# Fifteen small loads of 1 to 15 rows, each with its own semaphore, between the last two parts of w_down

## The chip, the cores and the metric

The kernel runs on one core of one Trainium2 chip. Such a core has five engines that run side by side, each from its own list of instructions: TensorE (PE in the profile; PEld is its loading of weights), VectorE (DVE), ScalarE (ACT), GpSimd (POOL) and SyncE (SP). Sixteen DMA engines move data between the chip's memory (HBM) and the on-chip memory (SBUF). Engines wait for each other, and for DMAs, on semaphores. The metric is the time of one execution in microseconds (us) on the device. Three runs of the kernel before took 1309.85 to 1310.14 us, the median is 1309.92 us.

## The reference

One decoding step of a transformer block, in float32, for a batch of 2 with one new position each: attention over a cache of 8192 positions in 32 heads of 128, and then a gated feed-forward layer. The model width D is 512, the inner width F of the feed-forward layer is 1792.

```
h  = x + attention(layernorm(x))        # q = layernorm(x) @ wq, then per batch and head:
                                        #   softmax(q . k_cache / sqrt(128)) @ v_cache
                                        # and the heads' outputs, side by side, @ wo
h2 = h + (silu(n @ w_gate) * (n @ w_up)) @ w_down,   n = layernorm(h)
```

k_cache and v_cache are 2 x 32 x 8192 x 128 numbers each. Every number of them is used once, so nearly all the traffic is cache.

## The kernel before, in words

The kernel is written by hand as five lists of steps, one for each engine. `do` adds a step to an engine's list, and gives it a semaphore to raise if one is named; `wait` adds a wait to the list. A DMA raises its semaphore by 16 in all when it has landed. `emit` writes the lists out in order. So each engine works strictly in the order in which its steps were added, and that of SyncE's loads is the order of the list `loads`.

The attention goes in 32 rounds (U = 32), two heads of one batch entry a round. A round reads 8 MB of k_cache and 8 MB of v_cache. VectorE multiplies the keys with the query (L418) and sums up (L427), TensorE helps with the softmax (L318 to L323) and multiplies the probabilities with the values (L328). There are two buffers for keys, `kslot`, and one for values, `vslot`; the last round's values go to a key buffer. SyncE waits until a buffer is free (`freed`, L579) and then issues the load into it (L580).

Behind the cache, in the same list, come the weights of the end: wo in three parts into `vslot` (5, 2 and 1 MB), w_gate and w_up in two parts each into a key buffer (1.75 MB each), and w_down in five parts into the other (`WD`, L190: 1 MB, 1 MB, 768 KB, 512 KB and 256 KB). Each part has a semaphore of its own, which `alone` makes, so that TensorE can start on a part as soon as it has landed. Before the first part of a weight SyncE waits for the step that frees its buffer (`after`, L202); the first part of w_down has to wait for TensorE's multiplication with the values of the last round (L328).

The end of the computation is a chain: the last round's output, the multiplication with wo (L477), a layernorm (L234 to L252), w_gate and w_up (L511), and w_down (L563), where TensorE waits for the semaphore of each part. VectorE copies the result (L574), and SyncE and ScalarE store one half of it each (L587). SyncE then waits for both stores and clears all semaphores, which are numbered without a gap (L593 to L596).

The lines around the change are those that put w_down's parts into the list of loads, and those that issue the list:

Of the kernel before, what the change touches and what calls it, by code (L numbers as in the profile page):

```python
# [13 lines left out]
class Program:  # L14
# [16 lines left out]
    def wait(self, engine, *points):  # L31
        for s, value in points:
            if self.known[engine].get(s, 0) < value:
                self.known[engine][s] = value
                self.steps[engine].append(lambda e, s=s, v=value: e.wait_ge(s, v))  # L35

    def do(self, engine, fn, sem=None, by=1):

        if sem is None:
            self.steps[engine].append(fn)  # L40
            return None
        self.count[sem] += by
        self.steps[engine].append(lambda e: fn(e).then_inc(sem, by))
        return sem, self.count[sem]
# [8 lines left out]
def decode_block(nc, x, k_cache, v_cache, wq, wo, w_gate, w_up, w_down, out):  # L53
    B, _, D = x.shape
    _, H, S, DH = k_cache.shape
# [21 lines left out]
    def sbuf(name, *shape, align=32):  # L77
        return nc.alloc_sbuf_tensor(name, list(shape), F32, align_bytes=align).ap()
# [51 lines left out]
    wait, do = g.wait, g.do  # L130
# [6 lines left out]
    def alone(name):  # L137
        return g.sem(name)
# [3 lines left out]
    landed = {}  # L142
    freed = {}
    loads = []
# [36 lines left out]
    for e, (c, n) in enumerate(WF):  # L181
        src, c0 = (w_gate, c) if c < DC else (w_up, c - DC)
        loads.append((
            ("wf", 0), e,
            wf_t[:, c * F : (c + n) * F],
            src.rearrange("(p c) f -> p (c f)", p=P)[:, c0 * F : (c0 + n) * F],
            alone(f"wf{e}"),
        ))
    wd_t = v_last
    WD = ((0, 4), (4, 4), (8, 3), (11, 2), (13, 1))  # L190
    for e, (c, n) in enumerate(WD):
        loads.append((
            ("wd", 0), e,
            wd_t[:, c * D : (c + n) * D],
            w_down.rearrange("(p c) m -> p (c m)", p=P)[:, c * D : (c + n) * D],
            alone(f"wd{e}"),
        ))
    count = {}
    for item, e, dst, src, sem in loads:
        count[sem] = count.get(sem, 0) + 16  # L200
# [31 lines left out]
    def layernorm(src, ready):  # L232
        wait("vector", *ready)
        p = do("vector", lambda e: e.bn_stats(stats, src), s_dve)  # L234
        wait("vector", p)
        p = do("vector", lambda e: e.bn_aggr(mv, stats), s_dve)
        wait("vector", p)
        p = do("vector", lambda e: e.tensor_scalar(ve, mv[:, 1:2], EPS, None, op0=OP.add), s_dve)
        wait("gpsimd", p)
        p = do("gpsimd", lambda e: e.tensor_tensor(rstd, ve, mhalf, op=OP.pow), s_pool)  # L240
        wait("vector", p)
        p = do(
            "vector",
            lambda e: e.tensor_scalar(y, src, mv[:, 0:1], rstd, op0=OP.subtract, op1=OP.mult),
            s_dve,
        )
        normed = p
        wait("tensor", p, ident_done)
        for c in range(DC):
            p = do(  # L250
                "tensor",
                lambda e, c=c: e.transpose(yt[:, c, :], y.rearrange("b (p c) -> b c p", c=DC)[:, c, :], ident[:B, :B]),  # L252
                s_pe if c == DC - 1 else None,
            )
        return normed, p

    _, p = layernorm(xs, [(x_in, 16)])
# [151 lines left out]
    for i in range(U):  # L409
        m, b = divmod(i, B)  # L410
        parts = 4 if i == 0 else 2
        n = NJ // parts
# [164 lines left out]
    for item, e_, dst, src, sem in loads:  # L577
        if item in after:
            wait("sync", freed[after[item]])  # L579
        do("sync", lambda e, dst=dst, src=src: e.dma_start(dst, src), sem, 16)  # L580
    stored = []
    for b, engine in enumerate(("sync", "scalar")):
        wait(engine, res_done)
# [52 lines left out]
```

## Time and profile before

| | us |
|---|---|
| median of three runs | 1309.92 (1309.85 to 1310.14) |
| the profiled execution, its own time | 1309.8 |
| its span, first to last instruction | 1308.5 |
| VectorE busy in it | 1131.7 |
| TensorE matmuls busy in it | 434.9 |
| loads of w_down issued | 1270.4 to 1276.9 |
| SyncE waits for the result, until | 1306.4 |

The profile is one execution, recorded by the hardware. Times within it count from the start of the span. The profile's page shows shares by engine and by slices of the span; the chain of waits follows the work that ended last back to what released it; the timeline shows instructions in order, with the time that an engine sat idle before them and what ended that in square brackets. "SPq" and "ACTq" are the sequencers of SyncE and ScalarE when they issue a DMA, and the length of such a line is the time that the issue took, not that of the transfer. The landing of a DMA is when its semaphore has been raised in full; the profile gives the time from issue to landing by load. The windows give the busy time of the engines, TensorE's granted clock, the share of time in which the DMA engines were busy, and GB/s, for a stretch.

### The profile page before, as it was taken

The numbers are of one execution on the slowest core, as the hardware profiler recorded it, in microseconds if no ns is written. First come the engines' busy times: TensorE is split into PE (matmuls) and PEld (weight loads), VectorE is DVE, ScalarE is ACT, GpSimd is POOL, SyncE is SP. The second block draws the span as 40 slices with busy tenths as digits, with TensorE's granted clock in tenths as the row PEclk, the third lists the DMA queues.
The fourth block names the chain that finished last, engine by engine and source line by source line (L and its number), as shares of the span: only waits on it lengthen the run. The fifth ranks groups of instructions, "written<-read, shape, count | busy, mean of one in ns | idle before, by whom it ended". The sixth has DMA issues, their size and how long they took to land.

```text
span 1308.5 us, 6711 instructions
## 1 busy us (share of the span) xinstructions
PE 434.9 (33%) x2952; PEld 135.4 (10%) x2952; DVE 1131.7 (86%) x250; ACT 80.4 (6%) x271; POOL 2.9 (0%) x13
## 2 busy tenths in 40 slices
PE   3633223333223333311333321233332233332177
PEld 1210001011001011100101100001100010110022
DVE  2999888889888889988888988888998888898841
ACT  0100000000000000000000000000000000000010
POOL 0000000000000000000000000000000000000000
PEclk9865566666556666656666656666655666665578
DMA  9999999999999999999999999999999999999998
GB/s 401 440 439 443 425 445 423 443 423 445 421 445 429 437 439 429 443 425 443 423 445 421 445 429 437 441 427 443 425 441 425 441 425 441 433 435 443 425 422 370
DMA packets 11550, 564.79 MB, mean 432 GB/s; under 512 B 1290, under 2 KB 1298, under 8 KB 1684
## 3 DMA queue, kind: packets, MB, share of 16 engines
q1 hardware_dynamic: 11528, 564.67, 99.7%
q8 instruction: 5, 0.08, 0.0%
q14 instruction: 5, 0.04, 0.0%
q10 hardware_dynamic: 12, 0.01, 0.0%
HBM read 564.66 MB, written 0.00 MB: 432 GB/s over the span
## 4 chain that ended last, share of the span: by engine, by line
DMA 56%; DVE 43%; PE 1%; issue 0%; SPq 0%; ACT 0%; DVEq 0%
DMA kslot<-in_A_k_cache_dram 48%; DVE kslot L418 21%; DVE s L427 21%; DMA kslot<-in_A_v_cache_dram 3%; DMA kslot<-in_B_w_down_dram 3%; DMA vslot<-in_A_wq_dram 2%; PE opart L328 1%; PE wide L291 0%; DVE gm L371 0%; DVE r L397 0%; PE bank L563 0%; SPq L580 0%; ACT qsb L302 0%; DVE kslot L574 0%; DVEq L35 0%
## 5 line engine op out<-in xcount | busy, mean ns | idle before, releaser
L418 DVE TENSOR_TENSOR kslot<-kslot,qsb 128x8192 f32<-128x8192 f32 (+1 forms) x66 | 555.9, 8422 | 126.8 <-DMA kslot<-in_A_k_cache_dram 103.7
L427 DVE TENSOR_REDUCE s<-kslot 128x64 f32<-128x8192 f32 (+1 forms) x66 | 555.5, 8417 | 0.1
L328 PE MATMUL opart<-vslot,pz 128*8 128x512 f32 x1984 | 285.2, 740 | 250.4 <-DMA vslot<-in_A_v_cache_dram 250.4
L320 PE MATMUL bank<-gm,nscale 1*64 1x1 f32 x64 | 11.8, 251 | 361.1 <-DVE gm L371 361.1
L328 PEld LDWEIGHTS opart<-vslot,pz 128*8 128x8 f32 x1984 | 55.2, 103 | 454.3 <-DMA vslot<-in_A_v_cache_dram 253.0
L318 PE MATMUL bank<-ident,m 128*1 128x128 f32 x64 | 18.7, 395 | 164.3 <-DVE m L435 164.3
L320 PEld LDWEIGHTS bank<-gm,nscale 1*64 1x64 f32 x64 | 9.1, 200 | 377.1 <-DVE gm L371 377.1
L340 PE MATMUL bank<-rdiag,osb 128*128 128x2 f32 x256 | 33.7, 254 | 23.6 <-ACT osb L404 23.6
L399 ACT ACTIVATE rdiag<-fold,r 128x8 f32<-128x8 f32 x32 | 9.6, 301 | 484.6 <-DVE r L397 484.6
L378 ACT ACTIVATE nb<-bank 128x1 f32<-128x1 f32 x32 | 5.5, 171 | 550.6 <-PE bank L321 550.6
L340 PEld LDWEIGHTS bank<-rdiag,osb 128*128 128x128 f32 x256 | 31.0, 191 | 53.3 <-ACT osb L404 53.3
L291 PE MATMUL wide<-vslot,osb 128*64 128x512 f32 x128 | 29.9, 631 | 17.2 <-DMA vslot<-in_A_wq_dram 17.2
L323 PE MATMUL bank<-rs,sides 128*128 128x1 f32 x64 | 18.8, 363 | 41.5 <-ACT pz L384 41.5
L384 ACT ACTIVATE pz<-s,nb 64x128 f32<-64x128 f32 x64 | 25.5, 399 | 1.4
L404 ACT ACTIVATE osb<-opart 128x512 f32<-128x512 f32 x32 | 19.1, 596 | 73.6 <-PE opart L328 73.6
L323 PEld LDWEIGHTS bank<-rs,sides 128*128 128x128 f32 x64 | 16.1, 313 | 44.2 <-ACT pz L384 44.2
L318 PEld LDWEIGHTS bank<-ident,m 128*1 128x1 f32 x64 | 2.7, 81 | 167.9 <-DVE m L435 167.9
L291 PEld LDWEIGHTS wide<-vslot,osb 128*64 128x64 f32 x128 | 10.4, 146 | 35.9 <-issue 35.9
L234 DVE BATCH_NORM_STATS2 ln_stats<-attn 2x6 f32<-2x512 f32 x1 | 0.7, 686 | 13.1 <-PE attn L490 13.1
L384 ACT ACTIVATION_READ_ACCUMULATOR pz<-s,nb 64x1 f32 x64 | 11.8, 184 | 0.0
L321 PE MATMUL bank<-gm,nscale 1*64 1x1 f32 x64 | 11.8, 251 | 0.0
L450 DVE TENSOR_TENSOR om<-oT,quarter 128x256 f32<-128x256 f32 x1 | 0.4, 425 | 11.4 <-ACT oT L406 11.4
(60 smaller groups left out, 105.1 us busy)
## 6 DMA issues: line engine op xcount, KB each, us to landing
kslot<-in_A_k_cache_dram SPq DMA_DIRECT2D x4, 2048.0 KB, 32.9
vslot<-in_A_wo_dram SPq DMA_DIRECT2D x1, 5120.0 KB, 22.0
kslot<-in_B_w_gate_dram SPq DMA_DIRECT2D x2, 1792.0 KB, 29.4
kslot<-in_B_w_up_dram SPq DMA_DIRECT2D x2, 1792.0 KB, 37.1
vslot<-in_A_wo_dram SPq DMA_DIRECT2D x1, 2048.0 KB, 26.5
kslot<-in_B_w_down_dram SPq DMA_DIRECT2D x2, 1024.0 KB, 30.0
vslot<-in_A_wo_dram SPq DMA_DIRECT2D x1, 1024.0 KB, 28.5
kslot<-in_B_w_down_dram SPq DMA_DIRECT2D x1, 768.0 KB, 32.1
```

The lines of the kernel that those rows point to most:

```text
L291: lambda e, ps=ps, c=c, k=k, m=m, b=b: e.matmul(ps[HALF[k]], xb[:, c * B + b, :], wqv[:, c, k, m : m + 4, :], start=(c == 0), stop=(c == D ...
L318: e.matmul(mrow, m1, ident, start=True, stop=True).then_inc(s_pe, 1)
L320: e.matmul(nb_ps[HALF[0]], nscale, gm[:, 0:1], start=True, stop=True)
L321: e.matmul(nb_ps[HALF[1]], nscale, gm[:, 1:2], start=True, stop=True).then_inc(s_pe, 1)
L323: e.matmul(den, sides.rearrange("p w a -> p (w a)"), rs, start=True, stop=True).then_inc(s_pe, 1)
L328: inst = e.matmul(opart[32 * t : 32 * t + 2 * W, :], pz[:, w, :], t_v[:, w * W * DH : (w + 1) * W * DH], start=(w < 4), stop=(w >= NW - 4),)
L340: inst = e.matmul(ot_ps, osb[:, a * DH : (a + 1) * DH], rdiag[:, a::W], start=(a == 0), stop=(a == W - 1))
L384: lambda e, k=k, h=h: e.activation(pz[h, :, k * W : (k + 1) * W], s[h].rearrange("p (w a) -> p w a", a=W), AF.Exp, bias=nb[h], scale=SCALE ...
L399: do("scalar", lambda e: e.activation(rdiag, diag, AF.Copy, scale=r))
L404: do("scalar", lambda e: e.activation(osb, opart, AF.Copy), s_act_pe)
L418: mult = do("vector", lambda e, kt=kt, qb=qb: e.tensor_tensor(kt, kt, qb, op=OP.mult), s_dve)
L427: lambda e, kt=kt, s=scores[i % 2][:, c * n : (c + 1) * n]: e.tensor_reduce(s, kt, axis=AX.X, op=OP.add),
```

## The change

After the list of loads is complete, fifteen loads are inserted ahead of its last entry, which is the fifth part of w_down. The n-th, for n from 1 to 15, reads the first 4 numbers (16 bytes) of the first n rows of w_down, and writes them to n partitions of a new tile, `probe`, in a column of its own. Each gets its own semaphore. The numbers are not used. SyncE issues them in its queue like all other loads, between w_down's fourth and fifth part, and nothing is waited for ahead of them. After all loads are issued, SyncE waits for all fifteen, and then, as before, for the result, to store its half.

```diff
+    probe = sbuf("probe", 16, 16, 4)
     wd_t = v_last
     WD = ((0, 4), (4, 4), (8, 3), (11, 2), (13, 1))
     for e, (c, n) in enumerate(WD):
...
             alone(f"wd{e}"),
         ))
+    PROBES = [("probe", n) for n in range(1, 16)]
+    for _, n in PROBES:
+        loads.insert(-1, (("probe", n), 0, probe[:n, n, :], w_down[:n, :4], alone(f"probe{n}")))
...
         do("sync", lambda e, dst=dst, src=src: e.dma_start(dst, src), sem, 16)
+    wait("sync", *(landed[item, 0] for item in PROBES))
```

On every engine but SyncE the instructions and their order stay the same. SyncE has 91 rows of them in place of 76, and fifteen waits more.

## The prediction

> **What bounds the kernel now.** I read the page first, for the shape of the whole run, then the chain of waits over the last 110 us, then the issues of the queue that the change enters, and last the windows around the landing of the load that the change precedes.
>
> ```profile
> span 1308.5 us, 6711 instructions
> PE 434.9 (33%) x2952; PEld 135.4 (10%) x2952; DVE 1131.7 (86%) x250; ACT 80.4 (6%) x271; POOL 2.9 (0%) x13
> DMA  9999999999999999999999999999999999999998
> ...
> q1 hardware_dynamic: 11528, 564.67, 99.7%
> ...
> q10 hardware_dynamic: 12, 0.01, 0.0%
> ...
> DMA 56%; DVE 43%; PE 1%; issue 0%; SPq 0%; ACT 0%; DVEq 0%
> ```
>
> Two things share the span: the 16 DMA engines are busy in every slice, and VectorE is busy for 86%. The long part (32 rounds of cache reading) is a ring of loads and VectorE work; the change touches nothing of it. Whatever it does happens after the last cache load, where the chain of waits reads, in order of time (start, length, what):
>
> ```profile
> 1217.99 42.43 DMA kslot<-in_A_v_cache_dram
> ...
> 1260.46 9.94 PE opart L328 x64
> ...
> 1270.42 0.33 SPq L580
> ...
> 1272.01 32.90 DMA kslot<-in_B_w_down_dram
> 1304.91 0.04 issue
> 1304.96 1.09 PE bank L563 x24
> 1306.05 0.02 issue
> 1306.07 0.29 DVE kslot L574
> ```
>
> The end is set by the stream of weights. From 1272.0 to 1304.9 the chain is nothing but the fourth part of w_down waiting for its turn behind the weights issued before it. TensorE then needs 1.09 us, VectorE 0.29 us. The issues of SyncE's queue (SPq), one line each, and the times from issue to landing:
>
> ```profile
> 1270.42 0.33 SPq L580 DMA_DIRECT2D kslot<-in_B_w_down_dram  x1
> 1270.79 0.43 SPq L580 DMA_DIRECT2D kslot<-in_B_w_down_dram  x1
> 1271.63 0.33 SPq L580 DMA_DIRECT2D kslot<-in_B_w_down_dram  x1
> 1272.01 2.74 SPq L580 DMA_DIRECT2D kslot<-in_B_w_down_dram  x1
> 1274.80 2.08 SPq L580 DMA_DIRECT2D kslot<-in_B_w_down_dram  x1
> 1306.39 0.64 SPq L587 DMA_DIRECT2D out_dram<-kslot  x1
> ```
>
> ```profile
> vslot<-in_A_wo_dram SPq DMA_DIRECT2D x1, 2048.0 KB, 26.5
> kslot<-in_B_w_down_dram SPq DMA_DIRECT2D x1, 512.0 KB, 32.9
> kslot<-in_B_w_down_dram SPq DMA_DIRECT2D x1, 256.0 KB, 30.7
> ```
>
> and SyncE's own waits:
>
> ```profile
> SPq L587 <- DVE kslot L574: 29.5, 1, 29.5
> SPq L35 <- DMA out_dram<-kslot: 1.3, 1, 1.3
> ```
>
> The fourth part lands at 1272.01 + 32.9 = 1304.9, the fifth (256 KB, the last) at 1274.80 + 30.7 = 1305.5. So the last load is issued 30 us before it is needed, and only its place in the queue decides when it lands. What the last landing releases, and the DMA engines around it:
>
> ```profile
> 1304.95 0.38 PEld L563 LDWEIGHTS bank<-kslot 128*32 128x32 f32 x16 [0.63 <-DMA kslot<-in_B_w_down_dram]
> 1305.58 0.16 PEld L563 LDWEIGHTS bank<-kslot 128*32 128x32 f32 x8 [0.25 <-DMA kslot<-in_B_w_down_dram]
> ```
>
> ```profile
> 1290.00:1303.00 13.00, 10.16 (x132) 3.70 (x124) 2.18 (x3) 0.54 (x1) 0.00 (x0) 0.87 1.00 420
> 1305.20:1305.60 0.40, 0.40 (x19) 0.15 (x12) 0.00 (x0) 0.00 (x0) 0.00 (x0) 1.00 0.00 0
> ```
>
> TensorE's weight loads wait 0.25 us for the last landing: a delay of it goes to the end one for one. The last two columns of the windows are the DMA share and GB/s: full, 420 GB/s, until 1303, and nothing from 1305.2 on, though the last part is known to have landed only at 1305.5. So about 0.3 us lie between the last packet and the semaphore.
>
> **The change, part by part.**
>
> *The place.* The 15 small loads stand behind the fourth part of w_down and before the fifth. All else keeps its order, so only the fifth part can be late: by a late issue, or by packets ahead of it in the DMA engines. Both are costed, and the larger decides.
>
> *Issue.* An issue in an unhindered queue takes 0.33 to 0.43 us for 128 rows, and 0.64 us for the four-row store. Another load of few rows:
>
> ```profile
> 0.73 0.56 ACTq L209 DMA_DIRECT2D xs<-in_A_x_dram  x1
> ```
>
> So I take the dearer 0.64 for each: 15 x 0.64 = 9.6 us, and the fifth part's issue would end at 1276.9 + 9.6 = 1286.5. Latest harmless end: the store lands 1.3 us after its issue ended, and 256 KB at 420 GB/s take 0.62 us, so 1305.5 - 1.3 - 0.6 = 1303.6. At 0.64 us each there are 17 us to spare.
>
> But the last two issues took 2.74 and 2.08 us: the queue had no room. When the first of these ended (1274.75), the loads not yet landed were two of w_o (the 2 MB one lands at 1250.89 + 26.5 = 1277.4, its issue is below), four of w_gate and w_up, and four of w_down: ten. Is room counted in loads or in packets? Packets: q1's 11528 are 80 loads x 144, and 8 of the store; 144 is 128 rows and 16 semaphore writes, 9 a DMA engine. q10 shows the small form: 12 packets for two rows of x and four of the store, that is one row and one semaphore write for each engine used. A small load of n rows thus puts 2 packets on each of n engines, where a part of w_down puts 9 on all.
>
> ```profile
> 1250.89 0.43 SPq L580 DMA_DIRECT2D vslot<-in_A_wo_dram  x1
> ...
> DMA to landing us min/median/max: 27.5/29.4/31.3
> ```
>
> If room is counted in packets, the worst engine has to free 15 x 2 + 9 = 39 places. The two parts of w_gate (the row above, issued at 1256.61 and 1257.00) land at 1284.1 and 1288.3, 4.2 us for 9 packets an engine. 39 / 9 x 4.2 = 18.2 us, and the fifth part's issue ends near 1276.9 + 18.2 = 1295.1, still 8.5 us ahead of 1303.6. Cost of the issue: 0. Its cover is the backlog of w_gate, w_up and w_down; if that is not enough, see the first rival.
>
> *Packets.* Ahead of the fifth part, the worst engine gets 15 rows and 15 semaphore writes. That all small loads begin on the same engine isn't shown by the profile; spread evenly it would be 120 / 16 = 7.5 of each. I take 15, the worse. Price of one semaphore write: the last two parts land 0.63 us apart (the weight loads that wait for them start at 1304.95 and 1305.58), and 256 KB at 420 GB/s are 0.62 us, so a semaphore write behind a big row costs about 0.01 us. Price of a 16-byte row: no more than a row of 2 KB, 0.63 / 9 = 0.07 us, no less than a semaphore write, 0.01. Far apart; I take the geometric middle, 0.026. Sum: 15 x (0.026 + 0.01) = 0.54 us. Bounds: 0 (the delayed engine isn't the last to finish) and 30 x 0.07 = 2.1 us.
>
> The Trainium skill, DMA: Bandwidth & Descriptors, section "Why a DMA increments its semaphore by 16 and not by 1", states that a transfer uses the largest number of engines up to 16 that divides its rows, always the lowest-numbered ones. By that rule the 15 is right; spread evenly, the sum would be 0.27 us. The packet count of q10 agrees with as many engines as rows; which engines they are no run here shows.
>
> *The wait at SyncE.* Fifteen waits stand before the store, nothing behind them but the store and the final waits. SyncE idles 29.5 us there. The small loads land before the fifth part, 0.8 us ahead of the copy's end (1306.36), and the waits are for them in order. Cost 0. If the cover were gone: 15 x 0.04 us, the gap between two issues, 0.6 us.
>
> *Semaphores.* The final clear spans 15 more. From the store's landing (1307.03 + 1.3 = 1308.3) to the end of the span are 0.2 us for everything, so at most 0.1 us more. I take 0. The tile of 16 partitions x 256 bytes is allocated last and moves nothing.
>
> *Sum.* 0 + 0.54 + 0 + 0: the span goes from 1308.5 to 1309.0, the profiled execution from 1309.8 to 1310.3. That execution stands 0.1 us under the median of the three runs shown, 1309.92; on the median, 1310.4 us, +0.04%.
>
> **The rivals.**
>
> *The issue comes late.* If the queue holds so many loads whatever their size, ten or eleven by the rows, the eleventh small load can only be issued when the fourth part of w_down is through, about 1304.9. Then four or five issues of 0.64 and 0.43 for the fifth part: it is issued by 1307.9, lands at 1307.9 + 1.3 + 0.6 = 1309.8, 4.3 us late. The same comes out if each issue simply costs the 2.08 us of the last: 16 x 2.08 = 33.3 us from 1274.80 is 1308.1, landing at 1310.0, 4.5 us late (with 2.74 each, 15 us). It decides from (1303.6 - 1274.8) / 16 = 1.8 us an issue, and the trace has issues on both sides of that. For it: the two long issues are the only ones of this queue under backlog. Against it: they ended at 1274.75 and 1276.88, when no load had just landed (1272.5 and 1277.4 are the nearest), so room came while a load was still running. Time: 1314.4 us.
>
> *The small loads run one after another in the DMA engine.* If a semaphore write has to wait for its row to be confirmed, and the next small load behind it, each costs the 0.3 us seen between last packet and landing: 15 x 0.33 = 5 us on the worst engine, 1314.9 us. It decides from 0.17 us each. Against it: the 0.63 us between the last two landings leave no room for such a stop. For it: there semaphore writes come 0.63 us apart, and nothing in this trace shows them closer.
>
> The Trainium skill, Perfetto Trace Analysis, section "DMA Instruction — HWDGE (DVE, Sync)", states that the last descriptor writes the semaphore only after the prior write is confirmed, which can take surprisingly long; it speaks for this rival, the 0.63 us against it as far as it goes. The same section has the issuing instruction last until its descriptors are generated, which speaks for room by packets, against the first rival.
>
> *The store waits for a small load.* A small load that becomes visible after 1306.4 holds SyncE's half of the store. By the store's own 1.3 us and several of them, about 1313 us. Little speaks for it, as they are ahead of the fifth part.
>
> *Faster.* The profile gives no way; a few parts in a hundred for a shifted instruction fetch or pairing.
>
> **How the numbers follow.** Hidden issue with short packets: 0.46. Late issue: 0.24. One after another: 0.20. Late store or another slower way: 0.07. Faster by more than 0.2%: 0.03. Within 0.2% (2.6 us, about what a measurement of this kernel can tell from no change) is the first alone: same 0.46, slower 0.24 + 0.20 + 0.07 = 0.51, faster 0.03. The predicted time is that of the likeliest single case, 1310.4; its own range is 1309.8 to 1312.0 (packets free, or 2.1 us). To hold 8 in 10 the range reaches to the rivals' 1314.4 and 1314.9, so to 1315.4; what lies beyond (longer stalls, faster) has under 2 in 10.
>
> **What the profile after would show.** Right: the small loads' issues in SPq are short or spread over the w_gate and w_up stretch, and the fifth part's issue ends well before 1303; the last two landings of w_down are 1.0 to 1.4 us apart in place of 0.63; the DMA share stays full until the last part. Late issue: long SPq lines up to 1305, the fifth part's time from issue to landing drops from 30.7 to about 2 us, and the DMA share falls to nothing before it. One after another: the fifth part issued early, but several us between the last two landings with the DMA share low. What would make the forecast wrong is the count of room in the queue, and the price of a 16-byte row, of which the trace of before has no example.

## The result, and the profile after

The changed kernel takes 1312.09 us (median of 17 runs, 1311.67 to 1312.63). The kernel before, timed beside it, takes 1309.97 us (1309.78 to 1310.55). That is 2.1 us more, a ratio of 1.0016 with a 95% interval of 1.0009 to 1.0022. The time lies in the stated range and just inside the 0.2% that were called no change. But it is 1.7 us above the predicted 1310.4, so a term of the sum was too small.

The page of the changed kernel, its span, the load queue and the chain:

```profile
span 1310.8 us, 6734 instructions
...
q1 hardware_dynamic: 11768, 564.67, 99.6%
...
DMA 54%; DVE 43%; SPq 2%; PE 1%; issue 0%; ACT 0%; DVEq 0%
```

The queue has 240 packets more: 120 rows and 120 semaphore writes, as costed. SyncE issues 96 DMAs in this profile, where the profile before has 81; the 91 and 76 rows given with the change are not counts of it. The share of SPq in the chain has grown from 0% to 2%. Its rows are the issues of w_down's parts and of the small loads, which here lead up to the fifth part; the chain's last piece before TensorE is again a landing. The chain of the end (start, length, what), then the issues of four of the small loads, the first and the last among them, and of the fifth part:

```profile
1270.54 0.04 issue
1270.58 0.44 SPq L584
...
1291.88 15.89 DMA kslot<-in_B_w_down_dram
1307.78 0.04 issue
1307.82 0.47 PE bank L567 x8
1308.29 0.02 issue
1308.31 0.29 DVE kslot L578
```

```profile
1275.27 0.33 SPq L584 DMA_DIRECT2D probe<-in_B_w_down_dram  x1
1285.51 1.56 SPq L584 DMA_DIRECT2D probe<-in_B_w_down_dram  x1
1289.24 1.55 SPq L584 DMA_DIRECT2D probe<-in_B_w_down_dram  x1
1290.83 1.01 SPq L584 DMA_DIRECT2D probe<-in_B_w_down_dram  x1
1291.88 0.49 SPq L584 DMA_DIRECT2D kslot<-in_B_w_down_dram  x1
...
kslot<-in_B_w_down_dram SPq DMA_DIRECT2D x1, 512.0 KB, 33.5
kslot<-in_B_w_down_dram SPq DMA_DIRECT2D x1, 256.0 KB, 15.9
probe<-in_B_w_down_dram SPq DMA_DIRECT2D x1, 0.2 KB, 16.8
```

The fifth part is issued at 1291.9, well ahead of the 1303.6 that would be late. Still it lands only at 1291.88 + 15.9 = 1307.8, and the last small load at 1290.83 + 16.8 = 1307.6. What TensorE's weight loads waited for, and the windows around it (share of the DMA engines and GB/s in the last two columns):

```profile
1305.39 0.38 PEld L567 LDWEIGHTS bank<-kslot 128*32 128x32 f32 x16 [0.65 <-DMA kslot<-in_B_w_down_dram]
1307.82 0.16 PEld L567 LDWEIGHTS bank<-kslot 128*32 128x32 f32 x8 [2.05 <-DMA kslot<-in_B_w_down_dram]
```

```profile
1303.00:1304.00 1.00, 0.36 (x16) 0.09 (x4) 0.00 (x0) 0.00 (x0) 0.00 (x0) 1.00 1.03 317
1304.00:1305.00 1.00, 0.85 (x24) 0.59 (x24) 0.00 (x0) 0.00 (x0) 0.00 (x0) 1.00 0.50 140
1305.00:1306.00 1.00, 0.62 (x17) 0.38 (x16) 0.00 (x0) 0.00 (x0) 0.00 (x0) 1.00 0.25 58
1306.00:1307.00 1.00, 0.03 (x4) 0.00 (x0) 0.00 (x0) 0.00 (x0) 0.00 (x0) 1.00 0.03 10
1307.00:1308.00 1.00, 0.18 (x8) 0.16 (x8) 0.00 (x0) 0.00 (x0) 0.00 (x0) 1.00 0.00 0
```

The wait for the last part grew from 0.25 to 2.05 us. In the last of these windows nothing is moved at all; in the one before, 10 GB/s. So it isn't data that TensorE waits for. The semaphore events of the trace tell what it is. Each row below is one load, and the time is that of the last of its DMA engines:

```
w_down part 4      1305.35
small load,  4 rows 1305.54      10 rows 1306.68
             5      1305.75      11      1306.86
             6      1305.93      12      1307.04
             7      1306.12      13      1307.22
             8      1306.31      14      1307.41
             9      1306.49      15      1307.59
w_down part 5      1307.78
```

From the load of 4 rows on the semaphores come one after the other, 0.185 us apart: 13 steps, 2.43 us (2.43 / 13 = 0.187). The trace also has the start and the length of every single packet, and these tell what stands in line. All 120 rows of 16 bytes and their semaphore writes of 4 bytes take 9 ns each. The last twelve rows start between 1305.01 and 1305.14, 12 ns apart, each with its semaphore write behind it, while the last twelve landings of small loads are spread over 1305.54 to 1307.59. The last packet of the fifth part ends at 1306.50, 1.28 us before the part lands; in the kernel before it is 0.33 us (1305.21 and 1305.54). So the packets go through quickly, and it is the raising of the semaphores behind them that comes in steps. The data of the fifth part are held up too, but less: 10 of its 128 rows of 2 KB take 0.17 to 1.21 us in place of 0.084.

In the kernel before the two parts landed 0.62 us apart, so 1.81 us of the 2.1 lie here. The remaining 0.3 us does not belong to this place. In the profiled run the last cache load was already issued 0.47 us later than before (1218.46 against 1217.99), and the last part of w_up, which also stands ahead of the small loads, landed 0.35 us later (1297.34 against 1296.99). What causes that was not found.

### The profile page after: what moved, and what is told of

Same layout as the page of the kernel before. It is cut to its first block, busy times and chain, and to the rows that moved or that the text cites. A ratio compares the mean times of both kernels' runs of the same rounds, so it can differ in the third digit from the quotient of the medians.

```text
span 1310.8 us, 6734 instructions
## 1 busy us (share of the span) xinstructions
PE 430.3 (33%) x2952; PEld 134.6 (10%) x2952; DVE 1131.7 (86%) x250; ACT 80.5 (6%) x271; POOL 2.9 (0%) x13
## 4 chain that ended last, share of the span: by engine, by line
DMA 54%; DVE 43%; SPq 2%; PE 1%; issue 0%; ACT 0%; DVEq 0%
DMA kslot<-in_A_k_cache_dram 48%; DVE kslot L422 21%; DVE s L431 21%; DMA kslot<-in_A_v_cache_dram 3%; DMA vslot<-in_A_wq_dram 2%; SPq L584 2%; DMA kslot<-in_B_w_down_dram 1%; PE opart L332 1%; PE wide L295 0%; DVE gm L375 0%; DVE r L401 0%; ACT qsb L306 0%; PE bank L567 0%; DVE kslot L578 0%; DVEq L35 0%
## 5 line engine op out<-in xcount | busy, mean ns | idle before, releaser
L515 PE MATMUL wide<-kslot,hT 128*32 128x448 f32 x64 | 9.5, 743 | 2.8 <-DMA kslot<-in_B_w_up_dram 2.5
L439 DVE TENSOR_REDUCE m<-s 128x1 f32<-128x128 f32 x32 | 9.2, 286 | 1.1
```

## The experiments

Theory A, from that table: a small load leaves a semaphore write right behind its row on each DMA engine that it uses; these are confirmed (the semaphore is seen to rise) one after another, 0.185 us each, and the next part's semaphore stands behind them. If the engine that finishes last has n small loads between the two parts, they land (n + 1) x 0.185 us apart, or 0.62 us where that is longer. The rivals: the fifteen semaphores and waits cost at SyncE (B); the 16-byte rows are dear (C). The diffs are against the changed kernel, shortened where "..." stands.

**One semaphore.**

```diff
+    probe_sem = alone("probe")
...
-        loads.insert(-1, (..., alone(f"probe{n}")))
+        loads.insert(-1, (..., probe_sem))
...
-    wait("sync", *(landed[item, 0] for item in PROBES))
+    wait("sync", landed[PROBES[-1], 0])
```

> The fifteen small loads as in the changed kernel, but all on one semaphore, with one wait on it in place of fifteen. Theory A (each small load puts a semaphore write behind its row on each engine that it uses, and these are confirmed one after another, 0.185 us each, as the landings in the changed kernel's trace stand apart): the number of semaphore writes is the same, so the fourth and the fifth part of w_down still land 2.4 us apart, and the time is 1.8 to 2.1 us over before. Theory B (fifteen semaphores cost at SyncE: fifteen waits ahead of the store, a longer clear): nearly all of it goes, at most 0.5 us over before.

Measured: 1312.09 us against 1310.05 us, ratio 1.0016 (1.0007 to 1.0025); the two parts land 2.35 us apart. B falls: fourteen semaphores and fourteen waits less change nothing that can be seen against the changed kernel's 1312.09.

**One load with all the rows.**

```diff
-    probe = sbuf("probe", 16, 16, 4)
+    probe = sbuf("probe", 16, 16, 8)
...
-    PROBES = [("probe", n) for n in range(1, 16)]
-    for _, n in PROBES:
-        loads.insert(-1, (("probe", n), 0, probe[:n, n, :], w_down[:n, :4], alone(f"probe{n}")))
+    PROBES = [("probe", 15)]
+    loads.insert(-1, (
+        ("probe", 15), 0, probe[:, 1:, :4],
+        w_down[:16, : 15 * 4].rearrange("p (a b) -> p a b", b=4), alone("probe15"),
+    ))
```

> One load in place of fifteen, of 16 partitions with 15 separate rows of 16 bytes each: 15 rows on every DMA engine, but one semaphore write. Theory A (semaphore writes in line): one confirmation more, the last two parts land 0.6 to 0.8 us apart, 0 to 0.3 us over before. Theory C (a row of 16 bytes is dear in itself, about 0.15 us each): as the changed kernel or more, 2.4 us apart, 1.8 to 2.3 us over before.

Measured: 1310.35 us against 1310.05 us, 1.0002 (0.9993 to 1.0011). The parts land 0.60 us apart, the small load 0.19 us after the fourth. Fifteen 16-byte rows on every engine are hidden in that one confirmation. C falls.

**Sixteen rows each.**

```diff
-        loads.insert(-1, (("probe", n), 0, probe[:n, n, :], w_down[:n, :4], alone(f"probe{n}")))
+        loads.insert(-1, (("probe", n), 0, probe[:, n, :], w_down[:16, :4], alone(f"probe{n}")))
```

> Fifteen loads of 16 rows each, so that all 16 DMA engines get 15 rows and 15 semaphore writes, the one that finishes last too (in the changed kernel it seems to get 12). Theory A: 16 x 0.185 = 3.0 us between the last two landings, 2.3 us over before, 2.3 to 2.6 with what else the changed kernel lost. If the count on the last engine does not matter: as the changed kernel, 2.4 us apart.

Measured: 1312.63 us against 1310.05 us, 1.0020 (1.0011 to 1.0029). The parts land 1305.58 and 1308.56, 2.98 us apart; 16 x 0.185 is 2.96. It is the number on the last engine that counts. TensorE's rows of this run:

```profile
1305.62 0.42 PEld L567 LDWEIGHTS bank<-kslot 128*32 128x32 f32 x16 [0.28 <-DMA kslot<-in_B_w_down_dram]
1308.60 0.16 PEld L567 LDWEIGHTS bank<-kslot 128*32 128x32 f32 x8 [2.56 <-DMA kslot<-in_B_w_down_dram]
```

**One row each.**

```diff
-        loads.insert(-1, (("probe", n), 0, probe[:n, n, :], w_down[:n, :4], alone(f"probe{n}")))
+        loads.insert(-1, (("probe", n), 0, probe[:1, n, :], w_down[:1, :4], alone(f"probe{n}")))
```

> Fifteen loads of one row each. If they all go to the first DMA engine (which by the changed kernel's landings finishes the fourth part of w_down some 2 us ahead of the slowest), theory A lets that engine land 16 x 0.185 = 3.0 us after its fourth part, about 0.7 us behind the slowest one: 0.5 to 1.0 us over before. If they are spread over the engines in turn: one more on each, 0 to 0.2 us over before.

Measured: 1310.58 us against 1310.05 us, 1.0003 (0.9994 to 1.0012). The fifteen land one after another, from 1303.65 to 1306.17 in steps of 0.18 us, so they are on one engine. The fourth part's first engine finished at 1303.47, one step ahead of the first small load, and its slowest at 1305.25, so the engine with the small loads was some 1.8 us ahead. The two parts land at 1305.25 and 1306.35, 1.10 us apart: of the 2.8 us only 0.5 us show. The difference in time, 0.5 us, is within the interval; the landings are what tells. TensorE waits for both parts as follows:

```profile
1305.29 0.38 PEld L567 LDWEIGHTS bank<-kslot 128*32 128x32 f32 x16 [0.67 <-DMA kslot<-in_B_w_down_dram]
1306.39 0.16 PEld L567 LDWEIGHTS bank<-kslot 128*32 128x32 f32 x8 [0.72 <-DMA kslot<-in_B_w_down_dram]
```

**Eight loads.**

```diff
-    PROBES = [("probe", n) for n in range(1, 16)]
+    PROBES = [("probe", n) for n in range(8, 16)]
```

> Only the eight loads of 8 to 15 rows. Theory A: the engine that finishes last gets 8 in place of 12; 9 x 0.185 = 1.7 us between the last two landings, 1.0 us over before (0.9 to 1.3). If the cost is a fixed one of having any small loads there: as the changed kernel, 2.1 us.

Measured: 1311.38 us against 1310.11 us, 1.0010 (1.0001 to 1.0019). The parts land at 1305.07 and 1306.74, 1.67 us apart, 9 x 0.185. The distance follows the number of loads. Here no row of the fifth part is held up (none takes over 0.084 us, and the last packet ends at 1305.49), and its semaphore still rises only 1.25 us later. The profiled execution does not show what that costs: TensorE was granted 0.50 of its clock from 1300 to 1306, was behind with its work, and no longer waited for the landing. This execution is the slowest of its eleven, 1311.86 us.

```profile
1302.90 4.68 PEld L567 LDWEIGHTS bank<-kslot 128*32 128x32 f32 x88
```

**Behind the last part.**

```diff
-        loads.insert(-1, (("probe", n), 0, ...))
+        loads.append((("probe", n), 0, ...))
...
-    wait("sync", *(landed[item, 0] for item in PROBES))
...
+    wait("sync", *(landed[item, 0] for item in PROBES))
     wait("sync", *stored)
```

> The fifteen small loads stand behind w_down's last part, and SyncE waits for them only after both stores are issued. Theory A (semaphore writes in line on an engine, nothing that matters behind them): the last two parts of w_down land 0.6 us apart as before, the small loads are all in 2.3 us after the last part, before the stores have landed: 0 to 0.4 us over before. If small loads in the queue cost wherever they stand: 1.8 us or more.

Measured: 1310.09 us against 1310.11 us, 1.0000 (0.9991 to 1.0009). The last small load is in at 1307.7, while the stores are on their way, and TensorE's waits are those of before:

```profile
1305.00 0.38 PEld L567 LDWEIGHTS bank<-kslot 128*32 128x32 f32 x16 [0.70 <-DMA kslot<-in_B_w_down_dram]
1305.63 0.16 PEld L567 LDWEIGHTS bank<-kslot 128*32 128x32 f32 x8 [0.26 <-DMA kslot<-in_B_w_down_dram]
```

The same loads, issues, semaphores and waits cost nothing that can be seen when nothing of importance lands behind them. No version in this study is faster than the kernel before by more than the runs can tell.

**Ahead of the first part.**

```diff
-        loads.insert(-1, (("probe", n), 0, ...))
+        loads.insert(-len(WD), (("probe", n), 0, ...))
```

> The fifteen small loads stand ahead of w_down's first part instead of its last. Theory A1 (an engine stops its data until the semaphore writes ahead are confirmed): the whole stream behind them is late, 1.8 to 2.1 us over before. Theory A2 (only semaphore writes are in line, and data behind them go on): the 2.4 us of confirmations pass while w_down's first part of 1 MB (2.4 us) is moved; all of w_down lands as before, 0 to 0.3 us over before.

Measured: 1311.70 us against 1310.11 us, 1.0013 (1.0003 to 1.0022). The first part of w_down lands at 1301.27, 1.85 us later than before (1299.42), and all parts after it as late, at their usual distances. Of this, 0.41 us is not the small loads' doing: the last part of w_up, ahead of them, is already that late (1297.40 against 1296.99). That leaves 1.44 us of the 12 x 0.185 = 2.22 us. So A1 is nearer: the stream behind is held up. It is not held up fully. From the last small load (1299.64) to the first part are 1.63 us, where the 1 MB takes 2.4 us, so some 0.8 us of its transfer had passed beside the confirmations. The packets show the holding up: most of the rows of 8 KB take 0.31 us as before, but some up to 1.44 us. TensorE's rows are later too. It was granted 0.50 of its clock from 1304 to 1306, and at the end it works through the last two parts in one group:

```profile
1303.77 1.48 PEld L567 LDWEIGHTS bank<-kslot 128*32 128x32 f32 x32 [1.55 <-DMA kslot<-in_B_w_down_dram]
1305.60 1.06 PEld L567 LDWEIGHTS bank<-kslot 128*32 128x32 f32 x24 [0.35 <-DMA kslot<-in_B_w_down_dram]
1306.83 1.10 PEld L567 LDWEIGHTS bank<-kslot 128*32 128x32 f32 x24 [0.18 <-DMA kslot<-in_B_w_down_dram]
```

**Rows of 2 KB.**

```diff
-    probe = sbuf("probe", 16, 16, 4)
...
-        loads.insert(-1, (("probe", n), 0, probe[:n, n, :], w_down[:n, :4], alone(f"probe{n}")))
+        c = F // P + n - 1
+        loads.insert(-1, (("probe", n), 0, wd_t[:16, c * D : (c + 1) * D], w_down[:16, :], alone(f"probe{n}")))
```

> Fifteen loads of 16 rows as in the run with all engines, but of 2 KB a row (the whole row of w_down, into unused space of w_down's buffer). The data alone are 491 KB, 1.2 us at 420 GB/s. Theory A with transfers under way while a semaphore write is confirmed: an engine needs 0.08 us for a row and 0.185 for the confirmation, the longer one counts, so the same as with 16-byte rows: 3.0 us between the last two landings, 2.3 us over before. If the row's time comes on top: 15 x 0.08 more, 4.2 us apart, 3.5 us over before. If it is bandwidth alone: 1.2 us over before.

Measured: 1318.34 us (1316.64 to 1318.77) against 1310.11 us, 1.0063 (1.0049 to 1.0077). None of the three expectations held. The profile, of the fastest run, shows a second effect: the fourth part, which stands ahead of the small loads, itself landed at 1308.70, more than 3 us late.

```profile
1308.74 0.63 PEld L567 LDWEIGHTS bank<-kslot 128*32 128x32 f32 x16 [3.70 <-DMA kslot<-in_B_w_down_dram]
1312.15 0.20 PEld L567 LDWEIGHTS bank<-kslot 128*32 128x32 f32 x8 [2.78 <-DMA kslot<-in_B_w_down_dram]
```

Engines that had finished the fourth part (the first at 1303.41) went on to the small loads, whose rows all lie in partitions 0 to 15, and the slow engines were held up in their work on the fourth part: its rows of 4 KB, 0.16 us each in the kernel before, take up to 0.66 us here. That the small loads hold them up is inferred from the times. Two runs ask whether the partitions are at fault: the same 32 KB and 16 semaphore writes a load, first over all 128 partitions (in shorter rows, 256 bytes), then in every eighth. Their diffs are against this run.

```diff
-        c = F // P + n - 1
-        loads.insert(-1, (("probe", n), 0, wd_t[:16, c * D : (c + 1) * D], w_down[:16, :], alone(f"probe{n}")))
+        c = F // P * D + n * 64
+        loads.insert(-1, (("probe", n), 0, wd_t[:, c : c + 64], w_down[:P, :64], alone(f"probe{n}")))
```

> The run with 2 KB rows was 8.2 us slower, not 2.3 or 3.5, and there the fourth part of w_down landed late as well. Its rows all went to partitions 0 to 15. Here each of the fifteen loads moves the same 32 KB and raises its semaphore on all 16 engines too, but as 128 rows of 256 bytes over all 128 partitions. Theory P (many engines writing to the same few partitions hinder each other, and what is behind them): the excess goes; semaphore writes in line alone give 3.0 us between the last two landings and 2.3 to 2.9 us over before. Theory Q (the bytes between the semaphore writes make the confirmations longer, 0.35 to 0.5 us each): as the run with 2 KB rows, 6 us or more over before.

Measured: 1313.25 us against 1310.19 us, 1.0023 (1.0013 to 1.0033). The excess of 5.6 us is gone but for 0.2 us above the expected 2.9. The fourth part lands at 1305.10, with none of its rows held up, and the last small load at 1307.89, 15 steps of 0.186 us. The fifth then comes not 0.19 but 0.96 us later, at 1308.85, and that is the issue:

```profile
1277.53 11.20 SPq L584 DMA_DIRECT2D kslot<-in_B_w_down_dram  x1
...
1305.01 1.42 SPq L584 DMA_DIRECT2D kslot<-in_B_w_down_dram  x1
...
kslot<-in_B_w_down_dram SPq DMA_DIRECT2D x1, 256.0 KB, 3.8
```

With 9 packets an engine in each small load, one issue takes 11 us, the fifth part is issued only at 1305.0, and it lands 3.8 us later. This is the late issue that the prediction's first rival feared, brought about by the number of packets and not by that of loads; the changed kernel does not reach it.

```diff
-        loads.insert(-1, (("probe", n), 0, wd_t[:16, c * D : (c + 1) * D], w_down[:16, :], alone(f"probe{n}")))
+        loads.insert(-1, (("probe", n), 0, wd_t[::8, c * D : (c + 1) * D], w_down[:16, :], alone(f"probe{n}")))
```

> As the run with 2 KB rows, 16 rows of 2 KB a load, but into every eighth partition (0, 8, up to 120) in place of 0 to 15. Theory P (few neighbouring partitions share a way into the memory): the rows are spread over more of it, the excess over 2.6 us falls from 5.6 us to less than half, 2.6 to 5 us over before, and the fourth part lands less late. Theory R (16 engines writing to 16 partitions that are not each engine's usual ones is what hurts, wherever they lie): 7 us or more over before.

Measured: 1314.93 us against 1310.19 us, 1.0037 (1.0023 to 1.0051): 4.7 us over before, in theory P's range, near its upper end. The fourth part lands at 1307.27, still late, by 2.2 us where the sixteen rows in neighbouring partitions made it 3.6 us late (each against the 1305.1 of the run over all partitions). Its rows of 4 KB take up to 0.53 us. Against the run with rows of 2 KB only the partitions differ, so it matters which partitions the engines write to. By what way they hinder each other no run shows.

The runs that tell on theory A, with the landings of the fourth and fifth part from the traces; n is the number of small loads on the engine that finished last. The run with one row each, whose small loads were on an engine that was ahead, and the run ahead of the first part are told above and do not fit the columns:

| run | n | (n + 1) x 0.185 | apart | over before |
|---|---|---|---|---|
| before | 0 | (0.62, the data) | 0.62 | |
| behind the last part | 0 | (0.62, the data) | 0.64 | 0.0 |
| one load | 1 | (0.62, the data) | 0.60 | 0.3 |
| eight loads | 8 | 1.67 | 1.67 | 1.3 |
| changed kernel | 12 | 2.41 | 2.43 | 2.1 |
| one semaphore | 12 | 2.41 | 2.35 | 2.0 |
| sixteen rows each | 15 | 2.96 | 2.98 | 2.6 |

"Over before" is 0.2 to 0.3 us more than "apart" less 0.62 in the rows from "one load" on. That is within the intervals of the ratios, and it stays open.

## Why the prediction was right or wrong

*The place, and that only the fifth part can be late:* right for the 1.81 us between the last two landings. The other 0.3 us, in the profile there ahead of the small loads already, has no cause found.

*Issue, 0:* right, and for the reason given. Room in the queue goes by packets. The issues from 1285.51 to 1289.24 and those before them show a period of 3.73 us for four small loads, 8 packets on the first engine, 0.466 us each; the prediction's 4.2 us for 9 is 0.467. The fifth part's issue ended at 1292.4 (1291.88 + 0.49), forecast 1295.1. The rival "the issue comes late" is ruled out for this kernel; loads of 9 packets an engine bring it about.

*Packets, 0.54:* this is the step that failed. The rows were taken for dear (0.026) and the semaphore writes for cheap (0.01). It is the other way round: fifteen rows under one semaphore leave the distance of the two parts at 0.60 us, while with a semaphore for every small row each of them comes 0.185 us after the one ahead of it. The 0.01 was read from the last two parts of before, where 0.62 us of data lie between two semaphore writes and hide the confirmation. The prediction had named that very gap in its second rival ("nothing in this trace shows them closer"), but did not carry it into the term. The term measures 1.81 us. That this lies under the upper bound of 2.1 us is luck, as the bound was 30 packets at 0.07 us, and the packets take 0.009. The whole time, 1312.09, is just above the 1312.0 at which the likeliest case's own range ended; it is in the stated range because that was widened for the rivals. Two signs that were to show the likeliest case did not come: the last two landings 1.0 to 1.4 us apart (2.43), and the DMA engines full until the last part (a share of 0.03 from 1306 to 1307). What came, an early issue and the landings far apart with the DMA engines nearly idle, was the sign named for "one after another".

*"I take 15, the worse":* one engine does get 15, as the landings in the run with one row each show, but in that run it was 1.8 us ahead of the slowest. The engine that ends last got 12. That the small loads do not lie on all engines alike thus softened the blow; with 15 on all, it is 2.6 us. The Trainium skill, DMA: Bandwidth & Descriptors, section "Why a DMA increments its semaphore by 16 and not by 1", has the lowest-numbered engines used; the traces agree so far: all fifteen one-row loads land on one engine, and the engine that ends last in the changed kernel has every small load from four rows on, 12 in all.

*The wait at SyncE, 0, and the semaphores, 0:* right. SyncE's store is issued 0.07 us after ScalarE's, and one semaphore in place of fifteen gains nothing:

```profile
1308.63 0.61 ACTq L592 DMA_DIRECT2D out_dram<-kslot  x1
1308.70 0.62 SPq L592 DMA_DIRECT2D out_dram<-kslot  x1
```

*The rival "one after another":* in the main this is what happened, at a smaller price. It was put at 0.33 us each, from the time between the last packet and the landing, and at 5 us in all; measured are 0.185 us, and 12 of them in place of 15. So the mechanism nearest to what the runs show was given 0.20, while the time came out between it and the likeliest case. One piece of it is not borne out: the next small load's packets do not wait, they follow after 12 ns, and only the semaphores come in line. The Trainium skill, Perfetto Trace Analysis, section "DMA Instruction — HWDGE (DVE, Sync)", has the semaphore written only after the prior write is confirmed. The steps of 0.185 us agree with that, but no run here separates the wait for the confirmation from the raising of the semaphore itself.

## What to carry to other kernels

In these runs each load's semaphore took 0.185 us on each DMA engine that the load used, and the semaphores of the loads behind it stood in the same line. Loads with more than that of data on each engine (here 256 KB over 16 engines, 0.62 us) hid it; eight to fifteen tiny ones ahead of a load that was waited for did not, so put such loads behind it, or make them one load. A cost read off a place where something else hides it is a lower bound, not a price.

## What the runs showed of the hardware that was not expected

- Semaphores of one DMA engine's loads rise 0.185 us apart when little data lie between them, though the packets, semaphore writes included, take 9 ns each.
- Transfers behind such a line are held up too, but not always: none with eight in line behind the fourth part, 10 of the fifth part's 128 rows in the changed kernel, 32 of 128 with fifteen on every engine. With the small loads ahead of w_down, 1.44 us of the 2.22 us came through to the whole of it.
- Loads of 16 rows of 2 KB slow down other transfers, by where the rows go: 8.2 us over before in partitions 0 to 15, 4.7 us in every eighth. With the same bytes in rows of 256 bytes over all 128 partitions it was 3.1 us.
- Room for issues is used up by packets: with 2 an engine, four issues every 3.73 us; with 9, one issue took 11.2 us.
